# Whole attention products, and second-layer matmuls shared out unevenly, in a fused attention and MLP kernel

## The chip, the cores and the metric

The kernel runs on one core of a Trainium2 chip. The metric is the device time of one execution in microseconds (us); of the kernel before there are three timed runs, and one further execution under the hardware profiler, from which the profile comes. Engines are named as in the profile: PE (TensorE), with PEld for its weight loads, DVE (VectorE), ACT (ScalarE), POOL (GpSimd) and SP, which only issues DMAs here. PSUM, the memory that PE writes, has eight banks, numbered 0 to 7, of 512 float32 columns in each of 128 partitions.

## The reference

Attention over 8 batches and 8 heads, sequence 576, head dimension 64, in which every score that lies more than tau below its row's maximum is dropped; then a two-layer network on the 4608 x 512 result.

```python
scores = scale * np.matmul(q, k.transpose(0, 1, 3, 2))
thresh = np.max(scores, axis=-1, keepdims=True) - tau
scores = np.where(scores >= thresh, scores, -1000000000.0)
scores = scores - np.max(scores, axis=-1, keepdims=True)
attn = np.exp(scores)
attn = attn / (np.sum(attn, axis=-1, keepdims=True) + 1e-09)
x = np.matmul(attn, v)               # heads side by side: 4608 x 512
...
h = x @ w_in                         # 512 -> 2048
g = h * np.clip(h + 3.0, 0.0, 6.0) / 6.0
out = g @ w_out                      # 2048 -> 512
```

## The kernel before, in words

**Units of work.** Two heads are a pair, two pairs a quad: 16 quads. A quad has nine slots. Slots 0 to 3 hold rows 0 to 511 of the first pair's queries, 128 rows of both heads in each; slots 4 to 7 those of the second pair; slot 8 the last 64 rows of all four heads. The 144 slots stand in one queue, and the loop over it (L527) writes out by hand, slot by slot, what each engine gets in its in-order queue. Nothing reorders it later.

**A slot's softmax.** Scores on PE in float32 (L287, contraction of 64 rows, so the array works in two halves of rows); row maxima on DVE while copying the scores out of PSUM (`sm_max`, L302); the mask on ACT (L309) and the exp with its row sum on ACT (L314); the reciprocal on DVE (L317); the normalising on POOL, which also turns them into bfloat16 (L322); and a transposing DMA (L330), or in the first slots a transpose on PE (L337), that makes pT.

**The attention product (AV).** `av` (L341 to L349) multiplies values with pT for one pair: ten matmuls for each range of columns, each with its own load of 64 weight columns, in two halves of the array's columns. `av_main` gives columns c0 to c0+w of the 512 main rows, `av_rest` the 64 last rows of both pairs of a quad. The product goes to a bank handed out by `bank()` (L212), which switches between banks 2 and 5 at each call, and DVE copies it to xT (L357) or xR (L367).

**The first layer (mm1).** An item is a bank full of h: eight matmuls of 256 columns (L381), or four of 512 for the rest rows (L376). ACT in even slots, DVE in odd ones, computes relu(h + 3) (L389, L391), and DVE multiplies the gate (`mm1_gate`, L404) into gbuf. From slot 22 on one item is done in each slot, as long as there is one. HB is bank 6, OB bank 7. Item and bank are chosen at the slot's start: bank 7 in an odd slot if the even slot before it had no mm2, otherwise bank 6.

**The second layer (mm2).** A tile is 128 tokens: 16 matmuls of 512 columns (L415), summed in bank 7, scaled out to SBUF by DVE (L423) and sent by SP (L436). A tile is cut into four parts of four matmuls; `second()` (L516) takes two parts in every even slot. What is over after the loop is done in a tail (from about 457 us on).

**The pace.** From slot 24 on an even and the following odd slot make a period. PE's order in it: mm1 of the even slot; the mm2 part; now and then a transpose of the rest of a quad's keys (kr, L257, into a bank from `bank()`); mm1 of the odd slot; an AV if one is due; and the scores of the next two slots, the even one's first. The scores of an even slot lie in banks 0, 1, 3 and 4, those of an odd slot in 1, 2, 4 and 5 (of banks 2 and 5 the first 256 columns, written by the last of the four steps). So banks 2 and 5 serve products, key transposes and scores.

**Who empties what, and when.** The kr transpose is issued in an even slot; its copies to kT (L222, two of 64 x 128 on ACT) are kept in `last_keys` and issued at the start of the odd slot. On ACT they then stand behind relu, two exps and the two masks of the even slot. Query transposes (L241) and output scaling that fall in an even slot are kept in `waiting` for the odd slot, where they are issued ahead of mm1's relu and gate.

**When a product is due.** `products` says after which slot: in quads from 2 on four products of 256 columns, two slots apart, and the rest two slots later; all fall in odd slots. Quads 0 and 1 have whole products of 512 columns.

Of the kernel before, what the change touches and what calls it, by code (L numbers as in the profile page):

```python
# [15 lines left out]
P = 128  # L16
# [4 lines left out]
def kernel(  # L21
# [11 lines left out]
    B, H, S, D = q.shape  # L33
# [4 lines left out]
    NI = d_ff // P  # L38
# [173 lines left out]
    def bank():  # L212
        nonlocal turn
        turn += 1
        return ps[:, (2, 5)[turn % 2], :]
# [135 lines left out]
    def av_main(pair, c0=0, w=512):  # L351
        b, hp = divmod(pair, NPAIR)
        if hp == c0 == 0:
            xT[b] = x_pool.tile([P, KI, 512], BF16, tag="xT", name="xT")
        pb = bank()[:, 0:w]
        av(pb, pair, pts[pair], slice(c0, c0 + w))
        return lambda: nc.vector.tensor_copy(out=xT[b][:, hp, c0:c0 + w], in_=pb)  # L357

    def av_rest(quad):
        b, g = divmod(quad, 2)  # L360
        pb = bank()
        for n in range(2):
            av(pb[:, n * 64:(n + 1) * 64], 2 * quad + n, ptr[quad], slice(n * 64, (n + 1) * 64))
        if b % 2 == 0 and g == 0:
            xR[b // 2] = x_pool.tile([P, KI, P], BF16, tag="xR", name="xR")
        o0 = 64 * (b % 2)
        return lambda: nc.vector.tensor_copy(out=xR[b // 2][:, 2 * g:2 * g + 2, o0:o0 + 64],  # L367
                                             in_=pb[:, 0:P].rearrange("p (a b) -> p a b", a=2))
# [39 lines left out]
    odd = {}  # L408
    o_ps = {}

    def mm2_part(bb, mt, part, ob=OB):
        if part == 0:
            o_ps[0] = ps[:, ob, :]
        for ni in range(part * 4, part * 4 + 4):
            nc.tensor.matmul(o_ps[0], gbuf[:, ni, mt * P:(mt + 1) * P], w_out_sb[:, ni, :],  # L415
                             start=(ni == 0), stop=(ni == NI - 1))

# [22 lines left out]
    def moe_of(b):  # L440
        items = []
        for c0, mts in (((0, (5, 6)), (None, (4,)), (256, (7, 8))) if b % 2 else ((0, (0, 1)), (256, (2, 3)))):
            for ni in range(0, NI, 4 if c0 is None else 2):
                items.append(((b, ni, c0), ()))
            items[-1] = (items[-1][0], [(b // 2, mt, part) for mt in mts for part in range(4)])
        if b % 2 and b < B - 1:
            items[10:14] = items[12:14] + items[10:12]
        elif b % 2:
            items[10:16] = items[12:16] + items[10:12]
        return items[0:8], items[8:]  # L450
# [45 lines left out]
    for quad in range(NQUAD):  # L496
        p0, p1 = 2 * quad, 2 * quad + 1
        if quad < NB:
            jobs = ((8, p0, 0, 512), (12, p1, 0, 512), (13, None, 0, 0))
        else:  # L500
            jobs = [(7 - quad % 2 + 2 * i, *of) for i, of in enumerate(
                ((p0, 0, 256), (p0, 256, 256), (p1, 0, 256), (p1, 256, 256), (None, 0, 0)))]
        for after, *of in jobs:
            products.setdefault(quad * NSLOT + after, []).append((quad, *of))

    def multiply(n):
        copies = []
        for of, pair, *columns in products.get(n, ()):
            copies.append(av_rest(of) if pair is None else av_main(pair, *columns))
            if of % 2 and pair is None:  # L510
                todo1.extend(moe_of(of // 2)[1])
            elif pair == 2 * of + 1 and of % 2 and columns[0] == 0:
                todo1.extend(moe_of(of // 2)[0])
        return copies

    def second():  # L516
        nonlocal pieces, bb, mt, part
        pieces = 2 if now % 2 == 0 and todo2 else 0
        for _ in range(pieces):
            bb, mt, part = todo2.pop(0)  # L520
            mm2_part(bb, mt, part)

    prev = None
    last_keys = []
    pieces = bb = mt = part = 0
    waiting = []
    for n, sl in enumerate(queue):  # L527
        quad, slot = sl.quad, sl.slot
        b, g = divmod(quad, 2)
        now = n  # L530
        if slot in (0, 4):
            pts[2 * quad + slot // 4] = pt_pool.tile([P, 9, 512], BF16, tag="pT", name="pT")
        if slot == 8:
            ptr[quad] = ptr_pool.tile([P, 9, P], BF16, tag="pR", name="pR")
        for ahead in {0: (1, 2), 9: (3,), 16: (4,)}.get(n, (quad + 2,) if quad > 2 and slot == (2 if quad == 3 else 0) else ()):
            if ahead < NQUAD:
                load_quad(ahead)
        if slot == 0 and g == 1 and b + 1 < B:
            load_v(b + 1)
        for copy in last_keys:  # L540
            copy()
        last_keys = []
        if 0 < n <= N1:
            for i in range(2):
                sm_exp(prev, i)
        if n + 1 < len(queue):
            sm_max(queue[n + 1])
        even = n >= N1 and n % 2 == 0
        if n > N1:
            sm_recip(prev)  # L550
        for copy in waiting:
            copy()
        waiting = []

        if todo1:
            item, then = todo1.pop(0)
            if n == len(queue) - 2:
                second()
            h = mm1(item, 0 if n == len(queue) - 1 else OB if n > N1 and n % 2 and not pieces else HB)
            todo2.extend(then)  # L560
        else:
            item = None
        if n >= N1:
            for copy in multiply(n):
                copy()
        if item:
            mm1_gate(item, h, mm1_relu(h, on_act=even))
        copies = pe_transpose(queue[n - 2]) if n > 1 and queue[n - 2].on_chip else None
        if prev is not None and n < N1:
            sm_recip(prev)  # L570
        if copies:
            copies()
        if n != len(queue) - 2:
            second()
        if n <= N1:
            for i in range(2):
                sm_mask(sl, i)
        if n == N1:
            sm_recip(prev)
        if n >= N1:  # L580
            for i in range(2):
                sm_exp(sl, i)
            if n + 1 < len(queue):
                for i in range(2):
                    sm_mask(queue[n + 1], i)
        if n < N1:
            for copy in multiply(n):
                copy()
        if part == 3:
            waiting.append(lambda tile=(bb, mt): late.extend(mm2_out(*tile, on_act=False)))  # L590
            part = 0
        evict = []
        for job, of in turns.get(n, ()):
            if job == "k":
                (last_keys if even else evict).append(transpose_k(of))
            elif job == "q":
                if of // 2 not in qkT:
                    alloc_qk(of // 2)
                (waiting if even else evict).append(transpose_q(of))
            else:  # L600
                (last_keys if even else evict).append(transpose_rest(of, of_k=of > 0))
        for out_of_psum in evict:
            if out_of_psum:
                out_of_psum()
        if n == 0:
            warm_up(8)
        if n <= N1:
            scores(n + 2)
        elif n % 2:
            for m in (n + 3, n + 2):  # L610
                if m < len(queue):
                    scores(m)
        if n < 8:
            warm_up(6)
        if n > 0:
            sm_norm(prev)
        flush()
        if n == 0:
            start(loads, 2)
        elif n not in (4, 12, 15, 18, 21) and not 23 < n < 30 and (n < 37 or n % 2 == 0):  # L620
            start(loads, 1)
        if n < 4 or 15 < n < 20 or n > 33:
            start(vcasts, 1 if n < N1 or n % 2 else 0)
        else:
            start(casts, 2 if n in (5, 8, 11, 14) or 21 < n < 28 else 1)
        prev = sl

    last = NQUAD - 1
    count = [1, 0 if todo2 and todo2[0][2] else 1]


    def last_out():
# [11 lines left out]
        todo2.extend(then)  # L644

    def rest2():
        while todo2:
            bb, mt, part = todo2.pop(0)
            mm2_part(bb, mt, part, ob=OB - count[1] % 2)
            if part == 3:  # L650
                flush()
                if (bb, mt) == (B // 2 - 1, 8):
                    last_out()
                else:
                    late.extend(mm2_out(bb, mt, on_act=(count[1] % 2 == 0)))
                count[1] += 1

    av_main(2 * last + 1, 0, 256)()
    for item in todo1:
        rest1(*item, on_act=False)  # L660
    sm_recip(prev)
# [47 lines left out]
```

## Time and profile before

| what | value |
|---|---|
| timed runs, median (lowest to highest) | 520.95 us (519.99 to 521.17) |
| profiled execution: its own time | 520.04 us |
| profiled execution: span of the records | 518.3 us |
| granted PE clock, mean | 0.999 |
| matmuls: scores (L287) | 1280, 174.0 us busy |
| matmuls: mm2 (L415) | 576, 134.1 us busy |
| matmuls: mm1 (L381) | 1024, 130.9 us busy |
| weight loads of values (L346) | 736, 110 ns each |
| relu on ACT (L389) / gate on DVE (L404) | 687 ns / 687 ns each |
| copy to xT, 256 columns / 512 columns (L357) | 419 ns / 690 ns each |
| ACT busy, DVE busy from 206 to 457 us (251.0 us) | 237.72 us, 235.44 us |

The profile was taken in one execution. Its page gives busy time by engine, the chain of work that ended last, and groups of equal instructions; the trace behind it can be asked for a timeline, in which a line holds start, duration, engine, source line, operation, output and inputs, shape and count, and in brackets the idle time before it with what ended it. Matmuls overlap in their pipeline, so the distance from one start to the next says more than a duration.

### The profile page before, as it was taken

The page shows a single profiled execution, that of the slowest core. Times are in us where ns is not written, and L with a number is a line of the kernel's source. Part 1 is how long each engine was busy: PE and PEld are TensorE (multiplying, and loading weights), DVE is VectorE, ACT ScalarE, POOL GpSimd, SP SyncE. Part 2 cuts the span into 40 slices and gives each one's busy share as a digit, 9 for nine tenths or more (in the row PEclk, how much of TensorE's full clock was granted, in tenths as well). Part 3 has the DMA queues.
Part 4 walks back from the last instruction along what each step waited for, and adds up shares of the span by engine and source line. Part 5 has one row for each costly group of instructions (what it writes and reads, how often), then busy time and mean ns, then how long its engine had stood idle before and what let it go on. Part 6 is the DMA issues. An engine that isn't in the chain of part 4 may idle for free.

```text
span 518.3 us, 12124 instructions
## 1 busy us (share of the span) xinstructions
PE 505.9 (98%) x4145; PEld 321.1 (62%) x4145; DVE 442.6 (85%) x1124; ACT 452.1 (87%) x980; POOL 299.3 (58%) x538
## 2 busy tenths in 40 slices
PE   8999999999999999999999999999999999999997
PEld 6765556666665666666665666666665666667563
DVE  3788887998999999999999999999999999887261
ACT  3999979999999999999999999999999999987060
POOL 1778869756676666657566656657566655552000
PEclk9999999999999999999999999999999999999999
DMA  5899899989999999999979998999999997564222
GB/s 132 123 173 163 142 161 156 174 147 171 167 178 157 170 162 183 177 170 179 177 150 164 157 199 159 166 166 178 167 163 168 178 178 123 114 113 71 77 67 61
DMA packets 314094, 78.77 MB, mean 152 GB/s; under 512 B 296624, under 2 KB 309168, under 8 KB 314032
## 3 DMA queue, kind: packets, MB, share of 16 engines
q1 hardware_dynamic: 294464, 67.90, 76.0%
q0 software_dynamic: 18368, 9.71, 15.1%
q8 instruction: 32, 0.52, 0.4%
q10 hardware_dynamic: 1200, 0.39, 0.3%
q14 instruction: 30, 0.25, 0.2%
HBM read 36.70 MB, written 9.44 MB: 89 GB/s over the span
## 4 chain that ended last, share of the span: by engine, by line
PE 81%; ACT 3%; DVE 2%; POOL 0%; issue 0%; POOLq 0%
PE ps L287 25%; PE ps L415 24%; PE ps L381 21%; PE ps L346 7%; PE ps L376 3%; ACT s L314 1%; PE ps L349 1%; ACT s L309 1%; DVE g L404 1%; ACT r L389 1%; DVE s L302 0%; DVE r L391 0%; POOL pn L322 0%; PE ps L257 0%; ACT kT L222 0%; DVE xT L357 0%
## 5 line engine op out<-in xcount | busy, mean ns | idle before, releaser
L322 POOL TENSOR_SCALAR pn<-s,rinv 128x576 bf16<-128x576 f32 x288 | 210.6, 743 | 19.0 <-issue 4.5
L302 DVE TENSOR_SCALAR_CACHE_REDUCE s<-ps 128x576 f32<-128x576 f32 x288 | 205.1, 749 | 17.6 <-PE ps L287 9.0
L309 ACT ACTIVATE s<-s,bias 128x576 f32<-128x576 f32 x288 | 205.8, 763 | 6.0 <-POOL bias L305 5.7
L314 ACT ACTIVATE s<-s 128x576 f32<-128x576 f32 x288 | 192.5, 671 | 0.3
L287 PE MATMUL ps<-kT,qT 64*128 64x384 f32 (+7 forms) x1280 | 174.0, 419 | 4.7 <-DVE s L302 3.8
L287 PEld LDWEIGHTS ps<-kT,qT 64*128 64x128 f32 (+1 forms) x1280 | 103.6, 175 | 59.3 <-issue 15.8
L415 PE MATMUL ps<-w_out_sb,g 128*128 128x512 bf16 x576 | 134.1, 379 | 0.0
L381 PE MATMUL ps<-xT,w_in_sb 128*128 128x256 bf16 x1024 | 130.9, 273 | 0.2 <-DVE g L404 0.2
L381 PEld LDWEIGHTS <-w_in_sb 128*128 128x128 bf16 x1024 | 95.5, 98 | 40.0 <-issue 20.8
L305 POOL TENSOR_SCALAR bias<-m 128x2 f32<-128x2 f32 x144 | 26.9, 187 | 154.5 <-DVE rinv L317 136.6
L404 DVE SCALAR_TENSOR_TENSOR g<-r,ps 128x512 bf16<-128x512 f32 x128 | 87.9, 687 | 15.2 <-ACT r L389 11.2
L415 PEld LDWEIGHTS <-g 128*128 128x128 bf16 x576 | 56.2, 98 | 56.8 <-issue 0.4
L389 ACT ACTIVATE r<-ps,three 128x512 f32<-128x512 f32 x81 | 55.6, 687 | 27.9 <-PE ps L381 23.8
L314 ACT ACTIVATION_READ_ACCUMULATOR s<-s 128x1 f32 x288 | 54.5, 189 | 0.0
L391 DVE TENSOR_SCALAR r<-ps 128x512 f32<-128x512 f32 x63 | 42.9, 681 | 0.0
L346 PE MATMUL ps<-pT,vm 128*64 128x256 bf16 (+1 forms) x480 | 39.1, 285 | 0.0
L346 PEld LDWEIGHTS <-vm 128*64 128x64 bf16 x736 | 27.3, 110 | 16.0 <-issue 14.3
L357 DVE CAST xT<-ps 128x256 bf16<-128x256 f32 (+1 forms) x60 | 26.3, 438 | 11.8 <-PE ps L349 11.8
L423 DVE TENSOR_SCALAR osb<-ps 128x512 f32<-128x512 f32 x31 | 20.9, 673 | 8.4 <-PE ps L415 8.4
L302 DVE DVE_READ_ACCUMULATOR s<-ps 128x1 f32 x288 | 23.9, 83 | 0.0
L317 DVE RECIPROCAL rinv<-rsum 128x2 f32<-128x2 f32 x144 | 23.0, 160 | 0.6 <-ACT s L314 0.6
L143 POOL DMA_DIRECT2D vm<-in_v_dram x28 | 21.4, 765 | 0.7 <-issue 0.7
(57 smaller groups left out, 259.4 us busy)
## 6 DMA issues: line engine op xcount, KB each, us to landing
out_dram<-osb SPq DMA_DIRECT2D x31, 256.0 KB, 2.9
nq<-in_q_dram SPq DMA_DIRECT2D x96, 72.0 KB, 3.5
km<-in_k_dram SPq DMA_DIRECT2D x96, 64.0 KB, 3.2
vm<-in_v_dram POOLq DMA_DIRECT2D x24, 128.0 KB, 4.0
km<-in_k_dram SPq DMA_DIRECT2D x16, 128.0 KB, 3.6
w_in_sb<-in_moe_w_in_dram POOLq DMA_DIRECT2D x16, 128.0 KB, 3.6
w_out_sb<-in_moe_w_out_dram POOLq DMA_DIRECT2D x16, 128.0 KB, 4.1
pT<-pn SPq DMA_TRANSPOSE x117, 4.0
```

The source lines that it names most:

```text
L287: nc.tensor.matmul(ps_flat[rows, c0:c0 + w], qT_of(pair)[a * 64:(a + 1) * 64, q0:q0 + rows.stop - rows.start], kT_of(pair)[a * 64:(a + 1) ...
L302: nc.vector.tensor_scalar(out=sl.s[:, i, :], in0=ps_flat[:, c0:c0 + S], scalar1=1.0, scalar2=None, op0=Alu.mult, op1=Alu.max, accum_out=sl ...
L305: nc.gpsimd.tensor_scalar(out=sl.bias[:], in0=sl.m[:], scalar1=-scale, scalar2=tau, op0=Alu.mult, op1=Alu.add)
L309: nc.scalar.activation(out=s, in_=s, func=Act.Prelu, bias=sl.bias[:, i:i + 1], scale=scale, alpha=REJECT)
L314: nc.scalar.activation(out=s, in_=s, func=Act.Exp, accum_out=sl.rsum[:, i:i + 1])
L322: nc.gpsimd.tensor_scalar(out=pn[:, i, :], in0=sl.s[:, i, :], scalar1=sl.rinv[:, i:i + 1], scalar2=1.0, op0=Alu.mult, op1=Alu.mult)
L346: nc.tensor.matmul(pb[a * 64:(a + 1) * 64, :], vm[:, 2 * hp + a, c * D:(c + 1) * D], pT[:, 5 * a + c, cols], start=(c == 0), stop=False)
L381: nc.tensor.matmul(ps[:, hb, n * 256:(n + 1) * 256], w_in_sb[:, ki, (ni + n) * P:(ni + n + 1) * P], xT[b][:, ki, c0:c0 + 256], start=(ki = ...
L389: nc.scalar.activation(out=r, in_=hps, func=Act.Relu, bias=three[:])
L391: nc.vector.tensor_scalar(out=r, in0=hps, scalar1=3.0, scalar2=0.0, op0=Alu.add, op1=Alu.max)
L404: nc.vector.scalar_tensor_tensor(out=out, in0=r, scalar=6.0, in1=hps, op0=Alu.min, op1=Alu.mult)
L415: nc.tensor.matmul(o_ps[0], gbuf[:, ni, mt * P:(mt + 1) * P], w_out_sb[:, ni, :], start=(ni == 0), stop=(ni == NI - 1))
```

## The change

Three things, all in the slot loop. First, in quads from 2 on a pair's product is made in one piece of 512 columns, and the quad's rest stands right behind the second pair's product; in every fourth quad (3, 7, 11, 15) the second pair keeps two pieces of 256. Second, `second()` no longer takes two parts of four: it looks at how many columns of product the next odd slot has, and takes 11, 9, 8, 6, 6 or 5 matmuls for 0, 128, 256, 384, 512 or 640 columns, never past the end of a tile; if fewer than the share and three more are left, it takes all of them. With the tiles of 16 this comes out mostly as 11 and 5, or 6 and 10. Third, to have room for them: in an odd slot with a whole product (`whole`) mm1 goes to that of banks 2 and 5 that `bank()` gave out last, and the product to the other one; a rest beside a whole product goes to bank 6. On DVE, relu and gate of the slot are now issued ahead of the copies of the products and of what was kept in `waiting`.

The diff:

```diff
--- before.py
+++ after.py
@@ -356,9 +356,9 @@
         av(pb, pair, pts[pair], slice(c0, c0 + w))
         return lambda: nc.vector.tensor_copy(out=xT[b][:, hp, c0:c0 + w], in_=pb)
 
-    def av_rest(quad):
+    def av_rest(quad, pb=None):
         b, g = divmod(quad, 2)
-        pb = bank()
+        pb = bank() if pb is None else pb
         for n in range(2):
             av(pb[:, n * 64:(n + 1) * 64], 2 * quad + n, ptr[quad], slice(n * 64, (n + 1) * 64))
         if b % 2 == 0 and g == 0:
@@ -408,10 +408,10 @@
     odd = {}
     o_ps = {}
 
-    def mm2_part(bb, mt, part, ob=OB):
-        if part == 0:
+    def mm2_part(bb, mt, n0, n1, ob=OB):
+        if n0 == 0:
             o_ps[0] = ps[:, ob, :]
-        for ni in range(part * 4, part * 4 + 4):
+        for ni in range(n0, n1):
             nc.tensor.matmul(o_ps[0], gbuf[:, ni, mt * P:(mt + 1) * P], w_out_sb[:, ni, :],
                              start=(ni == 0), stop=(ni == NI - 1))
 
@@ -442,7 +442,7 @@
         for c0, mts in (((0, (5, 6)), (None, (4,)), (256, (7, 8))) if b % 2 else ((0, (0, 1)), (256, (2, 3)))):
             for ni in range(0, NI, 4 if c0 is None else 2):
                 items.append(((b, ni, c0), ()))
-            items[-1] = (items[-1][0], [(b // 2, mt, part) for mt in mts for part in range(4)])
+            items[-1] = (items[-1][0], [(b // 2, mt) for mt in mts])
         if b % 2 and b < B - 1:
             items[10:14] = items[12:14] + items[10:12]
         elif b % 2:
@@ -498,31 +498,37 @@
         if quad < NB:
             jobs = ((8, p0, 0, 512), (12, p1, 0, 512), (13, None, 0, 0))
         else:
-            jobs = [(7 - quad % 2 + 2 * i, *of) for i, of in enumerate(
-                ((p0, 0, 256), (p0, 256, 256), (p1, 0, 256), (p1, 256, 256), (None, 0, 0)))]
+            jobs = (((9, p0, 0, 512), (13, p1, 0, 512), (13, None, 0, 0)) if quad % 2 == 0 else
+                    ((8, p0, 0, 512), (10, p1, 0, 256), (12, p1, 256, 256), (12, None, 0, 0)) if quad % 4 == 3 else
+                    ((8, p0, 0, 512), (12, p1, 0, 512), (12, None, 0, 0)))
         for after, *of in jobs:
             products.setdefault(quad * NSLOT + after, []).append((quad, *of))
 
     def multiply(n):
         copies = []
         for of, pair, *columns in products.get(n, ()):
-            copies.append(av_rest(of) if pair is None else av_main(pair, *columns))
+            copies.append(av_rest(of, ps[:, HB, :] if n > N1 and columns_at(n) > 512 else None) if pair is None else av_main(pair, *columns))
             if of % 2 and pair is None:
                 todo1.extend(moe_of(of // 2)[1])
             elif pair == 2 * of + 1 and of % 2 and columns[0] == 0:
                 todo1.extend(moe_of(of // 2)[0])
         return copies
 
+    def columns_at(n):
+        return sum(of[3] or P for of in products.get(n, ()))
+
     def second():
-        nonlocal pieces, bb, mt, part
-        pieces = 2 if now % 2 == 0 and todo2 else 0
-        for _ in range(pieces):
-            bb, mt, part = todo2.pop(0)
-            mm2_part(bb, mt, part)
+        nonlocal pieces, done
+        pieces = 0
+        if now % 2 == 0 and todo2:
+            share = {0: 11, 128: 9, 256: 8, 384: 6, 512: 6, 640: 5}[columns_at(now + 1)]
+            pieces = NI - done if NI - done < share + 3 else share
+            mm2_part(*todo2[0], done, done + pieces)
+            done += pieces
 
     prev = None
     last_keys = []
-    pieces = bb = mt = part = 0
+    pieces = done = 0
     waiting = []
     for n, sl in enumerate(queue):
         quad, slot = sl.quad, sl.slot
@@ -548,23 +554,28 @@
         even = n >= N1 and n % 2 == 0
         if n > N1:
             sm_recip(prev)
-        for copy in waiting:
-            copy()
-        waiting = []
+        if n <= N1:
+            for copy in waiting:
+                copy()
+            waiting = []
 
         if todo1:
             item, then = todo1.pop(0)
             if n == len(queue) - 2:
                 second()
-            h = mm1(item, 0 if n == len(queue) - 1 else OB if n > N1 and n % 2 and not pieces else HB)
+            whole = n > N1 and columns_at(n) >= 512
+            h = mm1(item, 0 if n == len(queue) - 1 else OB if n > N1 and n % 2 and not pieces else
+                    (2, 5)[turn % 2] if whole else HB)
             todo2.extend(then)
         else:
             item = None
-        if n >= N1:
-            for copy in multiply(n):
-                copy()
+        copies = multiply(n) if n >= N1 else []
         if item:
             mm1_gate(item, h, mm1_relu(h, on_act=even))
+        if n >= N1:
+            for copy in copies + waiting:
+                copy()
+            waiting = []
         copies = pe_transpose(queue[n - 2]) if n > 1 and queue[n - 2].on_chip else None
         if prev is not None and n < N1:
             sm_recip(prev)
@@ -586,9 +597,9 @@
         if n < N1:
             for copy in multiply(n):
                 copy()
-        if part == 3:
-            waiting.append(lambda tile=(bb, mt): late.extend(mm2_out(*tile, on_act=False)))
-            part = 0
+        if done == NI:
+            waiting.append(lambda tile=todo2.pop(0): late.extend(mm2_out(*tile, on_act=False)))
+            done = 0
         evict = []
         for job, of in turns.get(n, ()):
             if job == "k":
@@ -626,7 +637,7 @@
         prev = sl
 
     last = NQUAD - 1
-    count = [1, 0 if todo2 and todo2[0][2] else 1]
+    count = [1, 0 if done else 1]
 
 
     def last_out():
@@ -644,18 +655,21 @@
         todo2.extend(then)
 
     def rest2():
+        nonlocal done
         while todo2:
-            bb, mt, part = todo2.pop(0)
-            mm2_part(bb, mt, part, ob=OB - count[1] % 2)
-            if part == 3:
-                flush()
-                if (bb, mt) == (B // 2 - 1, 8):
-                    last_out()
-                else:
-                    late.extend(mm2_out(bb, mt, on_act=(count[1] % 2 == 0)))
-                count[1] += 1
+            bb, mt = todo2.pop(0)
+            mm2_part(bb, mt, done, NI, ob=OB - count[1] % 2)
+            done = 0
+            flush()
+            if (bb, mt) == (B // 2 - 1, 8):
+                last_out()
+            else:
+                late.extend(mm2_out(bb, mt, on_act=(count[1] % 2 == 0)))
+            count[1] += 1
 
     av_main(2 * last + 1, 0, 256)()
+    for copy in waiting:
+        copy()
     for item in todo1:
         rest1(*item, on_act=False)
     sm_recip(prev)
```

## Prediction

> **What bounds the kernel now.** I read the page's shares and chain first, then the groups by shape, then the timeline of one period.
>
> ```profile
> span 518.3 us, 12124 instructions
> PE 505.9 (98%) x4145; PEld 321.1 (62%) x4145; DVE 442.6 (85%) x1124; ACT 452.1 (87%) x980; POOL 299.3 (58%) x538
> ...
> PE 81%; ACT 3%; DVE 2%; POOL 0%; issue 0%; POOLq 0%
> ```
>
> TensorE is busy all the time and 81% of the chain is its own, so time added to or taken from its queue counts in full. ACT and DVE are near enough behind that a wait on either shows. From 102 to 457 us a period of two slots repeats; period starts lie 6.39 us apart most often. Here is one in which the rest of the keys (kr) is transposed:
>
> ```profile
> 217.72 1.05 PE L381 MATMUL ps<-xT,w_in_sb 128*128 128x256 bf16 x8
> 218.61 1.89 PE L415 MATMUL ps<-w_out_sb,g 128*128 128x512 bf16 x8
> 218.81 0.69 ACT L389 ACTIVATE r<-ps,three 128x512 f32<-128x512 f32 x1 [0.38 <-PE ps L381]
> 219.39 0.67 ACT L314 ACTIVATE s<-s 128x576 f32<-128x576 f32 x1
> 219.53 0.69 DVE L404 SCALAR_TENSOR_TENSOR g<-r,ps 128x512 bf16<-128x512 f32 x1
> 220.06 0.67 ACT L314 ACTIVATE s<-s 128x576 f32<-128x576 f32 x1
> 220.33 0.27 PE L257 MATMUL ps<-identf,kr 128*128 128x128 f32 x1
> 220.44 1.04 PE L381 MATMUL ps<-xT,w_in_sb 128*128 128x256 bf16 x8
> 220.72 1.43 ACT L309 ACTIVATE s<-s,bias 128x576 f32<-128x576 f32 x2
> 221.41 0.63 PE L346 MATMUL ps<-pT,vm 128*64 128x256 bf16 x8
> 222.06 0.52 ACT L222 COPY kT<-ps 64x128 f32<-64x128 f32 x2
> 222.08 2.21 PE L287 MATMUL ps<-kT,qT 64*128 64x384 f32 x16
> 224.22 0.28 PE L381 MATMUL ps<-xT,w_in_sb 128*128 128x256 bf16 x1
> ```
>
> Take differences of starts. First mm1 0.89, eight mm2 1.72 (0.216 each), kr 0.11, second mm1 0.97, attention product (AV) 0.67, scores 2.14. There is no gap on PE. Second thing to see: kr is written at 220.33, but ACT copies it out only at 222.06 to 222.58, because relu, two exps and two masks stand ahead of the copies in its order. Nobody minds today: the second mm1 goes to bank 6, the AV to the other one of banks 2 and 5.
>
> [...] mm1 (128x128) to AV (128x64) starts 202 ns apart where mm1 to mm1 is 109, AV to scores (64x128) 202 where 109 is usual; 93 ns for each change. [...] before has no mid-run PE gap above 1.0 us[...].
>
> **The change, part by part.** The same columns are multiplied; mm2 matmuls up to the end of the slot loop are 454 against 456, no difference of weight.
>
> *1. Fewer islands of AV.* Counted in the built instruction order, AV groups on PE (a rest beside a main product is one group) fall from 67 to 37. [...] its first pair takes 130 ns instead of 109: 93 + 21 = 114 ns. Three of the 30 lie before 100 us, where scores wait for DVE up to 1.0 us and nothing is gained. 27 x 0.114 = -3.1 us (ends -2 and -4.5). The 240 weight loads saved cost nothing here: pairs of 256 columns already start 106 to 109 ns apart, 256 columns' own pace.
>
> *2. The second mm1 of a period with a whole product moves to bank 2 or 5,* the one that was handed out last. Where kr stands just ahead of it, that is kr's own bank. In the built order the kr transpose takes the next bank in the turn, and the mm1 behind it, which waited for DVE before, now waits for ACT, by semaphore value for the second of the key copies (L222). This holds for 6 of the 12 kr periods after slot 29 (slots 30, 48, 66, 84, 102, 120), all with 5 mm2. Behind the waiting mm1 in PE's order stand the AV, the rests and all scores of that period. Its cost: ACT's chain from the first mm1 is unchanged (it idles 0.38 us for that mm1, so it can't be much earlier): copies end 222.58 - 217.72 = 4.86 us into the period, with 0.05 for the semaphore 4.91. PE would reach the mm1 after 0.89 + 5 x 0.216 + 0.11 = 2.08. Idle 2.83 us, nothing beside it on PE: 6 x 2.83 = +17.0 us. Ends: 2.0 each if ACT gets ahead, 3.2 if it lags: 12 to 19.
>
> *3. Uneven shares (11, 10, 6, 5).* A short share brings the second mm1 closer to the first. In bank 6 it waits for the gate (L404), which ends 2.5 us into the period (219.53 + 0.69 - 217.72). With 8 mm2 PE arrives at 2.61, covered; with 6 at 2.18, with 5 at 1.97. Whole products escape it by the other bank. Left are three periods with 6, a 256-column product and a rest (0.37 each, 1.1), and three with 5 and no product at all, because the tile had only five left (0.6, and about 0.25 more because DVE's row maxima then free the scores' banks late: 2.6).
>
> *4. The last scores of an odd slot reuse banks 2 and 5,* so they now wait for relu, gate and the 512-wide copy on DVE. DVE in a whole period from its start: two maxima, reciprocal, gate, two maxima, reciprocal to 3.9, relu to 4.6, gate to 5.2, copy (0.69 by the row of that form) to 5.85. The last quarter of the scores is due at 5.74 with 5 mm2, at 5.96 with 6, at 6.06 with a rest beside it. So 0.15 in each of six periods: 0.9. The change of order on DVE (relu and gate ahead of the copies, output scaling last) is what keeps this small, and one 0.69 copy replaces two of 0.42. Nobody waits for the output scaling: its bank is next written a whole mm1 later. A rest of an odd quad is read a period earlier; its transposing DMA lands some 4.0 us after issue, 2 us ahead of that, so I take nothing.
>
> Steps 3 and 4 together: 1.1 + 2.6 + 0.9 = +4.6 (from 1, if DVE keeps ahead, to 10, if its local overload carries over).
>
> Sum against the profiled execution (520.04 = span 518.3 and 1.7 around it): 520.04 - 3.1 + 17.0 + 4.6 = 538.5. The median of the runs, 520.95, is 0.9 higher; I give half of that: **539.0**.
>
> **Rivals.**
> *Weight loads matter after all (faster).* Place: every AV after slot 22. 240 loads fewer at 110 ns (groups by shape) are at most 26.4 us: 512.6. It would have to be worth over 77 ns a load to outweigh the 18.5 above. Against it: the pace of pairs, and PEld 62%.
> *The copies are off the path.* If ACT reached them within 2.08 us, step 2 is nothing: 522.0, about no change. Against it: 3.5 us of ACT work stand between relu's start and the copies' end, all in order.
> *DVE becomes the bound.* A whole period with output scaling and a transpose gives DVE some 7 us of work in 6.3 to 6.6 of PE; the next period gives back. If it doesn't, 0.4 us in each of 24 whole periods: 548.6. For it: DVE at 94% in the middle; against it: the following period has 11 mm2 and no copies.
> *The clock drops* in the 2.8 us gaps. [...]
>
> **How the numbers follow.** Forecast 0.74, DVE 0.09, clock 0.06, copies off the path 0.07, loads 0.04. The forecast's own ends (the bounds of its terms, not all at once) are 532 and 546; to leave no more than 2 in 10 out the range goes on to half of the two slow rivals: 532 to 549. About 0.2% (1 us) is what a measurement of this kernel can tell from no change. Faster by more: the loads, 0.04. Within: over half of copies off the path, 0.04. Slower: the rest, 0.92.
>
> **What would show it.** Right: among PE's waits a new row, L381 for ACT kT L222, six times about 2.8, 17 in total; AV groups of 512 at 1.07 us and 93 ns on both sides; periods with kr and a product near 9.4 us, others near 6.4; a few tenths at L381 for L404 and at L287 for L357. Wrong: no such row, or PE as dense as before; then only the islands are left. PE's clock below full after a gap would speak for the fourth rival, PE waits at L287 in most periods for the third.

## The result, and the profile after

The changed kernel takes 544.44 us (median of 4 runs: 543.04, 543.30, 545.59, 546.08). The kernel before, on the same chip, takes 520.47 us (median of 4: the three runs above and 519.98). The ratio is 1.046, with a 95% interval of 1.042 to 1.050: slower by 24 us, 5.4 us more than the forecast of 539.0 and inside the range. The profiled execution of after took 543.30 us, span 541.5, so what follows explains 23.3 us against the 520.04 of the profile before.

From the page of after, the span, the busy times, the granted clock in 40 slices and the shares of the chain:

```profile
span 541.5 us, 11662 instructions
...
PE 509.6 (94%) x3905; PEld 315.3 (58%) x3905; DVE 443.2 (82%) x1100; ACT 452.3 (84%) x980; POOL 299.3 (55%) x538
...
PEclk9999998989999999999999999999999999999999
...
PE 75%; ACT 7%; DVE 3%; issue 1%; POOL 0%; DVEq 0%; POOLq 0%
```

TensorE has 240 matmuls fewer, and yet is busy 3.7 us longer; its share of the chain falls from 81% to 75% and ACT's rises from 3% to 7%. So part of the chain that sets the end is now ACT's. The clock row, all nines before, has two dips, which come up below; they account for most of the longer busy time (two stretches at a clock of 0.50, 1.7 us each). PE's waits in after (engine, line, what it waited for: us in total, times, longest) name the place:

```profile
PE ps L381 <- ACT kT L222: 15.8, 6, 2.7
PE ps L287 <- DVE s L302: 4.6, 5, 1.7
...
PE ps L381 <- DVE g L404: 1.9, 6, 0.4
...
PE ps L415 <- DVE osb L423: 1.0, 1, 1.0
```

The first row did not exist before. The second was 3.8 us in before and the third 0.2, once; the last did not exist either. The timeline of one of the six periods of the first row (start, duration, engine, line):

```profile
350.29 1.05 PE L381 MATMUL ps<-xT,w_in_sb 128*128 128x256 bf16 x8
351.17 1.24 PE L415 MATMUL ps<-w_out_sb,g 128*128 128x512 bf16 x5
351.37 0.69 ACT L389 ACTIVATE r<-ps,three 128x512 f32<-128x512 f32 x1
...
352.27 0.33 PE L257 MATMUL ps<-identf,kr 128*128 128x128 f32 x1
...
353.29 1.43 ACT L309 ACTIVATE s<-s,bias 128x576 f32<-128x576 f32 x2
354.62 0.52 ACT L222 COPY kT<-ps 64x128 f32<-64x128 f32 x2
355.18 1.03 PE L381 MATMUL ps<-xT,w_in_sb 128*128 128x256 bf16 x8 [2.58 <-ACT kT L222]
```

The kr transpose is issued at 352.27; the mm1 behind it follows 2.91 us later, where it followed 0.11 us later in the period of before that the prediction shows. All the while ACT is not idle: relu, two exps, two masks, and only then the two copies that empty kr's bank. The mm1 starts 40 ns after them. The chain of waits runs through the same stretch (start, duration, engine, line):

```profile
351.37 0.69 ACT r L389
352.06 1.32 ACT s L314 x4
353.38 1.33 ACT s L309 x2
354.71 0.15 ACT kT L222
...
354.87 0.27 ACT kT L222
```

For 3.8 us the chain is ACT's (351.37 to 355.14). In the same stretch of before every piece of the chain is PE's.

Where the 23.3 us are, from period starts in the two traces (a period runs from one first mm1 to the next):

| part | us |
|---|---|
| six waits for the key copies, kr to mm1 2.91 to 2.94 us where it was 0.109 | +16.9 |
| two stretches of halved clock (0.50), 88.3 to 91.7 and 108.8 to 112.2 (1.7 each) | +3.4 |
| first period starts later, 75.42 against 74.85 | +0.6 |
| tail, a mm2 that waits for the output scaling once | +0.9 |
| the rest, which is what is left of the 23.3: fewer islands against small waits in the middle | +1.5 |

The six waits read 15.8 in the wait row because the ends of matmuls there are modelled; differences of starts are the safer measure. The 0.6 us of the first period is not a cost of the change: over the ten profiled executions shown here this start varies from 74.78 (e1) to 75.63 us (e4), and e5, which is the kernel before up to that point, has 75.33.

### The profile page after: what moved, and what is told of

Read it like the earlier page. It is cut to its first block, busy times and chain, and to the rows that moved or that the text cites. A ratio compares the mean times of both kernels' runs of the same rounds, so it can differ in the third digit from the quotient of the medians.

```text
span 541.5 us, 11662 instructions
## 1 busy us (share of the span) xinstructions
PE 509.6 (94%) x3905; PEld 315.3 (58%) x3905; DVE 443.2 (82%) x1100; ACT 452.3 (84%) x980; POOL 299.3 (55%) x538
## 4 chain that ended last, share of the span: by engine, by line
PE 75%; ACT 7%; DVE 3%; issue 1%; POOL 0%; DVEq 0%; POOLq 0%
PE ps L287 24%; PE ps L381 21%; PE ps L415 20%; PE ps L346 6%; PE ps L376 3%; ACT s L314 2%; ACT s L309 2%; ACT r L389 2%; DVE g L404 2%; PE ps L349 1%; ACT kT L222 1%; DVE s L302 1%; DVE r L391 0%; DVE xT L357 0%; POOL pn L322 0%
## 5 line engine op out<-in xcount | busy, mean ns | idle before, releaser
L322 POOL TENSOR_SCALAR pn<-s,rinv 128x576 bf16<-128x576 f32 x288 | 210.6, 743 | 19.3 <-issue 5.1
L287 PE MATMUL ps<-kT,qT 64*128 64x384 f32 (+7 forms) x1280 | 177.6, 421 | 5.7 <-DVE s L302 4.6
L381 PE MATMUL ps<-xT,w_in_sb 128*128 128x256 bf16 x1024 | 132.0, 275 | 17.8 <-ACT kT L222 15.8
L287 PEld LDWEIGHTS ps<-kT,qT 64*128 64x128 f32 (+1 forms) x1280 | 105.8, 176 | 64.5 <-DVE s L302 11.2
L404 DVE SCALAR_TENSOR_TENSOR g<-r,ps 128x512 bf16<-128x512 f32 x128 | 87.8, 686 | 16.6 <-ACT r L389 11.5
L346 PE MATMUL ps<-pT,vm 128*64 128x512 bf16 (+1 forms) x288 | 35.4, 368 | 0.0
L346 PEld LDWEIGHTS <-vm 128*64 128x64 bf16 x544 | 20.5, 111 | 16.4 <-issue 8.3
L357 DVE CAST xT<-ps 128x512 bf16<-128x512 f32 (+1 forms) x36 | 22.4, 626 | 2.1 <-PE ps L349 2.1
```

The source lines that it names most:

```text
L287: nc.tensor.matmul(ps_flat[rows, c0:c0 + w], qT_of(pair)[a * 64:(a + 1) * 64, q0:q0 + rows.stop - rows.start], kT_of(pair)[a * 64:(a + 1) ...
L322: nc.gpsimd.tensor_scalar(out=pn[:, i, :], in0=sl.s[:, i, :], scalar1=sl.rinv[:, i:i + 1], scalar2=1.0, op0=Alu.mult, op1=Alu.mult)
L346: nc.tensor.matmul(pb[a * 64:(a + 1) * 64, :], vm[:, 2 * hp + a, c * D:(c + 1) * D], pT[:, 5 * a + c, cols], start=(c == 0), stop=False)
L381: nc.tensor.matmul(ps[:, hb, n * 256:(n + 1) * 256], w_in_sb[:, ki, (ni + n) * P:(ni + n + 1) * P], xT[b][:, ki, c0:c0 + 256], start=(ki = ...
L404: nc.vector.scalar_tensor_tensor(out=out, in0=r, scalar=6.0, in1=hps, op0=Alu.min, op1=Alu.mult)
```

## The experiments

Each ratio is against runs of the kernel before that were timed beside the experiment: their median was 520.37 us beside e1 to e4, 520.65 beside e5 to e7 and 520.36 beside e8.

**e1: the keys' rest two slots earlier in even quads.** Everything else of the change is kept. In even quads from 4 on, kr moves to a period that has no whole product:

```diff
-    first_odd + (0, 2, 3, 4, 6)[i] if quad > 3 else ...
+    first_odd + (0, 2, 3 if quad % 2 else 1, 4, 6)[i] if quad > 3 else ...
```

> The changed kernel with one edit: in even quads from 4 on the transpose of the rest of the keys (kr) is issued two slots earlier, in a period without a product. My theory, that six kr periods cost 2.7 us each because the second mm1 goes to kr's bank and waits for ACT's copies: PE's wait for ACT kT L222 (15.8 us) is gone, no period of 9.5 us is left, and the halved clock after the first of these gaps goes with it; 525 us, 523 to 528. Rival, that DVE has become the bound (whole products and the new order on DVE): the time that PE is given back is lost to DVE waits at L287, and it stays above 535. Rival, that the wait only moves with kr: above 540.

Measured: 525.57 us (525.31 to 525.85), ratio 1.009, interval 1.008 to 1.011. 18.9 us of the 24 are gone. Among PE's waits are now:

```profile
PE ps L287 <- DVE s L302: 3.6, 5, 1.7
...
PE ps L381 <- DVE g L404: 1.9, 6, 0.4
```

The row of L222 is gone, and the 18 periods after which the pattern repeats take 117.2 us instead of 122.5 (before: 116.5). The second stretch of halved clock went with it (the first is still there: the scores from 85.92 us take 4.45 us by starts, the same ones 2.81 in before). So the meeting of kr and a whole product in one bank is what makes the change slow. Against before there remain, in the profiled execution, about 2.3 us up to 110 us, where that halved stretch lies, 2.6 in the middle and 0.9 in the tail.

**e2: the same meeting, a shorter wait.** Here the bank conflict is kept, but ACT does the key copies ahead of its two masks, right after the exps:

```diff
         if n >= N1:
...
+            if even and turns.get(n, [("", 0)])[0][0] == "rest":
+                transpose_rest(turns.pop(n)[0][1])()
```

> The changed kernel with one edit: the kr transpose stays in its slot and bank, and its two copies stand on ACT ahead of the two masks of the even slot instead of behind them. My theory, that the length of the wait is ACT's order and nothing else: the six waits of mm1 for kT L222 shrink by the two masks, 1.33 us, from 2.7 to about 1.4 each (8.4 in all), and the time falls by 8 us, more by some 2 if no gap is left that halves the clock: 535 us, 533 to 538. Rival, that the wait is for the bank's state and not for ACT's order: no change, 543 to 546.

Measured: 535.43 us (533.95 to 535.68), ratio 1.028 (1.026 to 1.030). From the timeline of e2:

```profile
347.50 0.52 ACT L222 COPY kT<-ps 64x128 f32<-64x128 f32 x2
348.04 1.44 ACT L309 ACTIVATE s<-s,bias 128x576 f32<-128x576 f32 x2
348.07 1.03 PE L381 MATMUL ps<-xT,w_in_sb 128*128 128x256 bf16 x8 [1.25 <-ACT kT L222]
```

The masks now follow the copies, and the mm1 waits 1.25 us instead of 2.58; the row totals 7.8 instead of 15.8. The difference, 1.33 us, is what the masks took ahead of the copies in the timeline of after (353.29 to 354.62). So the length of the wait is set by what stands ahead of the copies in ACT's order.

**e5: the meeting alone.** The kernel before, with one thing of the change: the mm1 behind kr goes to kr's bank, in all 12 periods.

```diff
-            h = mm1(item, 0 if n == len(queue) - 1 else OB if n > N1 and n % 2 and not pieces else HB)
+            h = mm1(item, 0 if n == len(queue) - 1 else OB if n > N1 and n % 2 and not pieces else
+                    (2, 5)[turn % 2] if n > N1 and any(job == "rest" for job, _ in turns.get(n - 1, ())) else HB)
```

> The kernel before with the disputed conflict alone: in the twelve odd slots that follow a kr transpose, mm1 goes to that one of banks 2 and 5 that kr has just been given, instead of bank 6; products, shares and DVE's order stay. My theory, that this bank is the cost, whatever else is in the period: mm1 waits for ACT's second copy, which ends 4.86 us into the period, 4.91 with the semaphore, where PE arrives at 0.89 + 8 x 0.216 + 0.11 = 2.73, so 2.18 us in each of 12 periods, 26 us: 546.5 us, 543 to 550, more by 1.7 us for each gap that halves the clock. Rival, that the periods before have slack that takes up part of it, as ACT's 0.38 us of idle time: under 540.

Measured: 555.18 us (555.01 to 556.03), ratio 1.067 (1.065 to 1.069), above the expected 546.5 by what the expectation adds for each halving of the clock: with five halved stretches of 1.7 us it comes to 555.0. From e5, one wait in the timeline of PE, the row of waits and the clock:

```profile
139.42 0.27 PE L257 MATMUL ps<-identf,kr 128*128 128x128 f32 x1
141.71 1.03 PE L381 MATMUL ps<-xT,w_in_sb 128*128 128x256 bf16 x8 [2.02 <-ACT kT L222]
143.26 3.78 PE L287 MATMUL ps<-kT,qT 64*64 64x384 f32 x24
```

```profile
PE ps L381 <- ACT kT L222: 24.2, 12, 2.0
```

```profile
PEclk9999999999899998999998999999899998999999
```

By starts each mm1 is 2.29 us behind kr instead of 0.109: 2.18 x 12 = 26.2 us. The remaining 8.3 us (555.2 - 520.65 - 26.2) go with five stretches of halved clock, 1.7 us each; the scores in the last line of the timeline run for the most part in one of them (142.85 to 146.26 us, at a clock of 0.50), and take 3.71 us by starts instead of the 2.31 of before. Each of these five follows a wait of 2.02 us, shorter than those of the change (2.58 to 2.67).

**e3: whole products alone.** The kernel before with the change's jobs of 512 columns only; eight mm2 in every period, banks and DVE's order as before.

```diff
-            jobs = [(7 - quad % 2 + 2 * i, *of) for i, of in enumerate(
-                ((p0, 0, 256), (p0, 256, 256), (p1, 0, 256), (p1, 256, 256), (None, 0, 0)))]
+            jobs = (((9, p0, 0, 512), (13, p1, 0, 512), (13, None, 0, 0)) if quad % 2 == 0 else
+                    ((8, p0, 0, 512), (10, p1, 0, 256), (12, p1, 256, 256), (12, None, 0, 0)) if quad % 4 == 3 else
+                    ((8, p0, 0, 512), (12, p1, 0, 512), (12, None, 0, 0)))
```

> The kernel before with one part of the change alone: whole products of 512 columns with the rest behind them, as in the changed kernel, but eight mm2 in each even slot, mm1 in banks 6 and 7 as before, and DVE's order of before. The periods are then uneven on PE: about 6.9 us with a whole product, 5.7 without. My theory: 27 islands fewer are worth 3.1 us; ACT, which needs 5.9 us a period, takes back 0.2 us in about half of the periods (1 to 5 us in all): 520 us, 517 to 523, so no change that matters, and no wait for kT L222 on PE. Rival, that unlike periods are costly and the change had to even them out: every long one is lost in full against the short ones, 0.5 us in each of 56 periods, and it is over 535. Rival, that the weight loads saved are worth much: under 512.

Measured: 530.57 us (528.59 to 531.83), ratio 1.019 (1.016 to 1.022). Neither what was expected nor a rival came true. Three periods of e3 in a row, busy time of each engine in each (us and instructions; the columns are named in the first line):

```profile
core 0: us, PE busy (x) PEld busy (x) DVE busy (x) ACT busy (x) POOL busy (x), PEclk, DMA share, GB/s
202.37:208.79 6.42, 6.21 (x41) 4.20 (x40) 5.71 (x15) 6.39 (x16) 4.43 (x8) 1.00 1.01 146
208.79:215.75 6.96, 6.96 (x51) 4.19 (x51) 5.96 (x16) 6.93 (x15) 4.09 (x8) 1.00 0.92 182
215.75:221.92 6.17, 6.12 (x41) 4.19 (x40) 6.13 (x16) 5.23 (x13) 3.65 (x7) 1.00 0.70 122
```

The second has a whole product and PE is busy all through it; it takes 0.57 us more than the usual 6.39. The first and the third have no product. Their matmuls at their own pace need 5.72 us (the prediction's 0.89 + 1.72 + 0.97 + 2.14), but they take 6.42 and 6.17. In the first ACT is busy for 6.39 us; in the third ACT has time to spare (5.23) and DVE is the full one, 6.13 us. So a short period does not give back all that its neighbour took: 18 periods take 119.1 us instead of 116.5. Whole products alone gain nothing here. That ACT and DVE hold the short periods is read from their busy times; no run took work off either to prove it. Not all of the 10.2 us is the periods' either: the profiled execution has a mean clock of 0.995, and the four runs lie in the order of their mean clocks, from 528.59 us at 0.998 to 531.83 at 0.992.

**e7: islands doubled.** The prediction costs an island of AV at 93 + 21 ns: one change of tile shape more than is there anyway, and a slow first pair. In e7 each 256-column product of the kernel before is made in two of 128, one ahead of the odd slot's mm1 and one behind it: 52 more islands, 520 more weight loads, the same columns.

```diff
+    def av_early(n):
+        for _, pair, *columns in products.get(n, ()):
+            if pair is not None and columns[1] == 256:
...
+                early[pair, c0] = pb = bank()[:, 0:256]
+                av(pb[:, 0:128], pair, pts[pair], slice(c0, c0 + 128))
...
+            if n > N1 + 6:
+                av_early(n)
```

> The kernel before with 52 more islands of attention product: from slot 29 on each product of 256 columns is made in two of 128, one ahead of the odd slot's mm1 and one behind it, in the same bank and with one copy as before; this takes twice the weight loads (520 more). My theory[...]: mm2 to product and product to mm1 are two changes of tiling at 93 ns and a slow first pair at 21, 207 ns for each, so 52 x 0.207 = 10.8 us: 531 us, 529 to 534. Rival, that weight loads are on the path: 520 loads of 110 ns more, up to 57 us, over 540 even at half of that. [...]

Measured: 531.84 us (531.08 to 532.01), ratio 1.022 (1.020 to 1.024): 11.2 us for 52 islands, 0.215 us each, where two changes of tile shape (2 x 93 ns) and a slow first pair (21 ns) make 0.207. From its timeline (in this kernel mm1 is L399 and mm2 L433):

```profile
209.05 1.67 PE L433 MATMUL ps<-w_out_sb,g 128*128 128x512 bf16 x7
210.65 0.41 PE L346 MATMUL ps<-pT,vm 128*64 128x128 bf16 x8
...
211.06 1.05 PE L399 MATMUL ps<-xT,w_in_sb 128*128 128x256 bf16 x8
212.03 0.41 PE L346 MATMUL ps<-pT,vm 128*64 128x128 bf16 x8
...
212.43 2.21 PE L287 MATMUL ps<-kT,qT 64*128 64x384 f32 x16
```

No wait stands in these lines: the periods are 0.24 us longer, and changes of shape are all that was added to PE beside the weight loads. The loads cost nothing that shows: after the first, pairs of 128 columns start 52 to 53 ns apart, half of the 106 ns of 256 columns in before, though each pair has its two loads as well.

**e6: DVE's order.** e1 with DVE's old order: the copies of the products, and what was kept in `waiting`, again ahead of relu and gate.

```diff
-            if n <= N1:
-                for copy in waiting:
-                    copy()
-                waiting = []
+            for copy in waiting:
+                copy()
+            waiting = []
...
+        for copy in copies:
+            copy()
         if item:
             mm1_gate(item, h, mm1_relu(h, on_act=even))
-        if n >= N1:
-            for copy in copies + waiting:
-                copy()
-            waiting = []
```

> The first experiment (kr two slots earlier, 525.6 us) with DVE's order of before: output scaling and kept copies ahead of mm1, the copy of the product ahead of relu and gate. My theory: DVE waits for a product of 512 columns to end (4.2 us into a period) before relu and gate, so the last scores, which need gate and bank, come 0.3 to 0.5 us late in each of 24 periods with a whole product: 533 us, 529 to 537, with PE waits at L287 for L404. The first periods before 110 us get back up to 1 us. Rival, that the order on DVE doesn't matter, because the waits at the scores are for row maxima: 524 to 527.

Measured: 536.45 us (536.17 to 537.65), ratio 1.031 (1.029 to 1.033), 10.9 us above e1. Waits of PE and then of its weight loads in e6:

```profile
PE ps L287 <- DVE g L404: 3.7, 10, 0.6
```

```profile
PEld ps L287 <- DVE g L404: 13.4, 22, 1.1
```

e1 has no such row. The last scores of an odd slot reuse the bank of its mm1; with the 512-wide copy and the output scaling ahead of the gate on DVE, that bank comes free late, and whole-product periods take 7.1 to 7.2 us instead of 6.5. So DVE's new order, one half of the third part of the change, is what keeps whole products bearable in e1.

**e4 and e8: can it be mended?** e4 is e1 with the small waits for the gate taken out: 8 mm2 for 384 columns, a share of 8 where neither this nor the next odd slot has a product, and quad 2 in pieces of 256.

```diff
-            share = {0: 11, 128: 9, 256: 8, 384: 6, 512: 6, 640: 5}[columns_at(now + 1)]
+            share = {0: 11, 128: 9, 256: 8, 384: 8, 512: 6, 640: 5}[columns_at(now + 1)]
+            if not done and columns_at(now + 1) == columns_at(now + 3) == 0:
+                share = 8
...
```

> The first of these experiments with two more edits: two periods without a product that follow each other, and those with 256 columns and a rest, take eight mm2 each instead of 11 and 5 or 6 and 10; and quad 2, before mm2 has started, keeps its pieces of 256 columns as in the kernel before. My theory: the waits of mm1 for gate L404 in bank 6 (about 0.6 in three periods and 0.4 in three) go, 3 us, and the 2 us go that the first periods lost against the kernel before, with the halved clock there: 520.5 us, 518 to 523, no better than the kernel before by more than 0.5%. Rival, that the saving in islands comes through once the waits are gone: 517 or less. Rival, DVE as the bound: over 526.

Measured: 525.66 us (525.18 to 527.38), ratio 1.010 (1.008 to 1.012): a miss, no better than e1. The waits for L404 shrink from 1.9 to 0.3 us, but the periods hardly do: the three of 6.63, 6.42 and 6.37 us became 6.70, 6.20 and 6.43, and the pair of 6.64 and 6.04 became 6.20 and 6.42 twice, 6.36 and 6.26 once. The short ones stop at about 6.2 us as in e3. Also one period takes 8.08 us, in which PE waits for the DMA that brings the transposed rest:

```profile
PE ps L346 <- DMA pR<-pn: 1.3, 1, 1.3
```

e8 is e1 with the start and the tail as in the kernel before: quad 2 in pieces of 256, DVE's old order for the slots below 30 and for slot 141, and the tail's copies first.

```diff
-            if n <= N1:
+            if n < 30 or n == len(queue) - 3:
                 for copy in waiting:
                     copy()
...
```

> The first experiment (kr two slots earlier, 525.6 us) with its first and last periods as in the kernel before: quad 2 keeps its pieces of 256 columns, and DVE has its old order up to slot 29 and in slot 141. My theory of what is left there, read from period starts: 2.3 us are lost ahead of 110 us, where PE waits for DVE or for the halved clock, 0.9 after the slot loop, where mm2 waits for an output scaling, and some 2 in between, where small waits outweigh the islands saved. The first two go: 522.4 us, 521.5 to 523.5, still not faster than the kernel before. Rival, that the loss is spread over all periods: 525 or more. Rival, that with these gone the islands show: under 520.

Measured: 524.91 us (523.89 to 526.13), ratio 1.009 (1.008 to 1.011): a miss too. Its profiled execution, 523.89, is 2.0 under that of e1. The tail is back at the length of before and the start within 0.4 us of it, but one period takes 7.83 us. Its weight loads wait for the same DMA; the row of the matmul behind them (1.1 us, once) names a gate on DVE that ended at the same moment. The waits of PE's weight loads in e8:

```profile
PEld L346 <- DMA pR<-pn: 2.1, 3, 1.5
```

So a rest that is read a period earlier has no slack left when its DMA is slow; the spread over runs fits that, but only one run of each has a trace. No version here beats the kernel before.

## Why the prediction was right, and where it was short

*What bounds the kernel.* Right: the long waits put on PE or taken off it counted in full (e1, e2, e5).

*Step 1, islands (-3.1).* The forecast takes 114 ns for an island between mm1 and scores: one change of shape (93) more than mm1 to scores has anyway, which start 225 ns apart at 78.6 us in before, and a first pair of 130 ns instead of 109. The price held: 0.215 us measured for an extra island between mm2 and mm1 in e7, with two changes of shape, against 0.207 from the same terms. The gain itself can't be seen alone: in e3, which has it, longer periods outweigh it. Weight loads are worth nothing here, as said: in after, AV pairs of 512 columns start 213 ns apart, twice the 106 of a 256-column pair.

*Step 2, kr's bank (+17.0).* Right in mechanism, place and size: six times, slots as listed, 2.82 us each by starts, 16.9 in all, in periods of 9.52 us where 9.4 was said. (ACT's work from relu's start to the copies' end is 3.77 us by the prediction's own lines, 218.81 to 222.58, not the 3.5 given there under the second rival; the sum did not use it.) e1 takes it out, e2 shortens it by what ACT does first, e5 makes it without the rest.

*Step 3, uneven shares (1.1 + 2.6).* Right. The periods with 6 mm2, 256 columns and a rest are 0.35 longer than PE's own pace (0.37 was said), those with 5 and no product 0.96 (0.85 was said). From the timeline of PE in e1, such a period (the trace lacks the record of one of its five mm2):

```profile
201.78 1.05 PE L381 MATMUL ps<-xT,w_in_sb 128*128 128x256 bf16 x8
202.88 1.03 PE L415 MATMUL ps<-w_out_sb,g 128*128 128x512 bf16 x4
204.33 1.03 PE L381 MATMUL ps<-xT,w_in_sb 128*128 128x256 bf16 x8 [0.42 <-DVE g L404]
205.29 2.60 PE L287 MATMUL ps<-kT,qT 64*128 64x384 f32 x16
207.82 1.05 PE L381 MATMUL ps<-xT,w_in_sb 128*128 128x256 bf16 x8
```

Both halves are there: 0.42 for the gate ahead of the second mm1 (0.58 by starts, 0.6 said), and scores that take 2.53 us by starts instead of 2.14. What the step missed is that taking these waits out gains next to nothing (e4): what PE no longer waits for here it loses in the neighbour.

*Step 4, scores behind DVE (+0.9).* Right in place, and a little short in size, in the middle of the run: the six periods with 5 mm2 and a whole product but no rest are 0.24 over PE's pace (0.15 was said). But "nobody waits for the output scaling" failed once: at slot 142 the next tile's mm2 begins early and waits for it, as the timeline of after shows.

```profile
485.07 0.68 DVE L423 TENSOR_SCALAR osb<-ps 128x512 f32<-128x512 f32 x1
...
485.80 1.46 PE L415 MATMUL ps<-w_out_sb,g 128*128 128x512 bf16 x6 [0.97 <-DVE osb L423]
```

That is the tail's 0.9 us. "I take nothing" for the rest's earlier reading was right for after, which has no wait for that DMA; with the long waits taken out (in e1 by 0.3 us, in e4 by 1.3, in e8 by up to 1.5 at the weight loads) it is no longer free. In before that DMA lands 4.4 us after issue (median of the row of pR), not the 4.0 of the prediction.

*The sum.* Steps 1 to 4 gave +18.5; the six waits, the rest of the middle and the tail come to 19.3. The forecast was inside its range, but it has no term for the clock: "The clock drops" was a rival at 0.06, and the trace of before, where PE has no wait above 1.0 us in the middle of the run, could not show what a longer gap would do. It came true in part. In the trace of after it happened twice, of which only one at a gap of step 2:

```profile
103.58:108.76 5.18, 2.51 (x18) 1.68 (x18) 3.42 (x11) 5.11 (x12) 3.09 (x7) 1.00 1.10 178
108.76:112.18 3.42, 3.42 (x19) 1.52 (x19) 1.38 (x2) 2.46 (x6) 0.49 (x1) 0.50 0.89 154
112.18:114.73 2.55, 2.55 (x39) 1.77 (x35) 1.57 (x3) 0.00 (x0) 0.00 (x0) 1.00 0.74 127
```

These are three stretches of one period, columns as above: PE half idle while it waits, then 3.42 us at a clock of 0.50 (PE busy throughout, at half pace), then full speed. The other stretch, 88.3 to 91.7, follows a wait of the scores for DVE at 84.9, 1.68 us long where before has 1.0; e1 and e2 have it too (scores of 4.45 and 4.03 us by starts behind the same wait of 1.68). The mean clocks of the four runs are 0.994, 0.994, 0.987 and 0.987; each such stretch lowers the mean by 0.5 x 3.42 / 541 = 0.003, so by this sum two runs had two of them and two had four. That would put the second two 3.4 us above the first; they are 2.7 above. Only one run has a trace, so this is an inference. Two stretches (3.4 us), the start (0.6, which varies from run to run) and the tail (0.9) come to what the forecast lacked against the profiled execution, 543.3 - 538.5 = 4.8. So the clock was the largest thing missed, and the nearness of 539.0 to 544.44 owes something to luck: six waits of this kind (2.58 to 2.67 us) were followed by one halved stretch in the profiled execution, and twelve in e5 (2.02 us) by five.

*The other rivals.* Loads: refuted by the pace of pairs, and by e7. Copies off the path: refuted by the row of L222. DVE as the bound: not in after, whose waits at L287 for DVE total 4.8 us; e6 shows that with the old order it would have cost 10.9.

*What became of the aim.* e1 and e3 differ by 5.0 us; e1 has the other banks, DVE's new order, the uneven shares and the earlier kr, and e3 has not. Under uneven shares the old DVE order costs 10.9. How much of the 5.0 belongs to the shares alone was not tried. Even e1, which has no bank conflict, stays 5.2 us behind before, 1.009 (1.008 to 1.011): PE was full already, and in the middle of the run the saving of fewer islands is smaller than the waits that uneven periods bring (18 periods in 117.2 us, 116.5 before).

## What to carry to other kernels

Before moving a matmul to another bank, ask who still has to read that bank and what stands ahead of that reader in its engine's order: here 0.5 us of copies behind relu, two exps and two masks cost 2.8 us six times, and moving one transpose by two slots took back 18.9 us. Moving PE's work from one period to the next did not pay where PE alone did not set the length of both: in e3 the shortened periods met an engine that was full (ACT at 6.39 of 6.42 us, DVE at 6.13 of 6.17). A price read from single lines (an island, a bank's wait) held to a few per cent; what was missed were effects that no line of the trace before could show, the clock first of all.

## What the runs showed of the hardware

In these traces the clock fell to half after some waits of PE and not after others. Three such stretches show a clock of 0.50, with PE busy all through: 88.28 to 91.70 and 108.76 to 112.18 us in after (3.42 us each), 142.85 to 146.26 in e5 (3.41). In e5 all twelve waits for L222 are 2.02 us, by modelled ends, and five are followed by slow scores: those from 143.26, 207.49, 300.30, 399.41 and 463.57 us take 3.64 to 3.94 us by starts, those behind the other seven waits 2.45 to 2.77. In after, one of the six waits of 2.58 to 2.67 us is followed by a halved clock, and the wait of 1.68 us at 84.9 is followed by one too; in e2 none of the six waits of 1.25 to 1.33 us is. So the length of the wait did not decide it alone; what else counts was not shown. Each halved stretch cost about 1.7 us: 8.3 us for five in e5, and in e2 the one run at a mean clock of 1.000 is 1.3 to 1.7 us faster than the three at 0.997.
